# LayerNorm's scale split between x and the residual, a weight-conversion step on ScalarE, softmax reciprocals on GpSimd

## The chip, the cores and the metric

The kernel runs on one core of a Trainium2 chip. A core has five engines, each with its own in-order queue: TensorE (PE, with its weight loads shown as PEld), VectorE (DVE), ScalarE (ACT), GpSimd (POOL) and SyncE (SP), which here only issues DMAs. The metric is the device time of the one core in microseconds (us).

## The reference

Three stages on 8 x 576 = 4608 tokens, 512 wide:

```python
# 1 attention in blocks of 64 tokens, 8 heads of 64
scores = (1/8) * q_c @ k_c.T ; attn = exp(scores - max)
out = (attn / (sum(attn) + 1e-9)) @ v_c          # -> x [4608, 512]
# 2 LayerNorm, an MLP 512 -> 2048 -> 512, residual
xn = (x - mu) / sqrt(var + 1e-06) * g_ln
x2 = x + maximum(xn @ w_ch1, 0) @ w_ch2
# 3 gated MLP 512 -> 1024 -> 512 with a depthwise convolution over 3 tokens
h = maximum(x2 @ w_in, 0) ; c = conv3(h, conv_w)
y = (h * sigmoid(c)) @ w_out
```

q, k, v and g_ln arrive as float32, the four weights as 64-bit floats that the kernel turns into float32 itself.

## The kernel before

Tokens go in 36 tiles of 128 and in 9 slabs of 512 (four tiles). Every large product takes both operands as a high and a low part and adds three matmuls (`mm3`, lines 114 to 117): low*high, high*low, high*high. The first MLP product uses a two-by-two scheme with seven products, numbered 1 to 7, in place of eight; each slab has 28 slots (4 groups G of 7 products), and each product is 12 matmuls.

The program has three phases. In the first, attention for all tiles and the first MLP product; the result goes to DRAM (`hd`). In the second (`Down`, lines 719 to 746), the second product and the residual (`finish`, lines 812 to 820). In the third, the gated MLP (`Gate`).

What the change touches lies in the first phase. Before slab 0 can start, a start phase must do the attention of tiles 0 to 3 and convert half of the weights of `w_ch1`; the other half is converted during the first slots of slab 0. The order of the start is written out by hand in `START` (lines 18 to 41): each token is a letter and a number, up to `|` issued one after the other, and behind it in lists that run after slots 0, 1, 2, ... of slab 0. As engines are in order, this list is the order of each queue. The letters:

- `W` loads a 512 KB piece of a weight block (four blocks of four pieces; pieces 0 to 7 are needed for the start). `a` (ACT, line 135) takes the upper bits, `t` (line 141) the lowest three bits out of the low word, `m` (line 147) and `n` (line 153) put bits and sign together on DVE, `g` (ACT, line 313) multiplies by LayerNorm's weight, one value per partition from `g_sb`. `s` (DVE) makes the sums that the seven products need, `h` (ACT, line 338) and `l` (DVE, line 158) split into high and low.
- `L` loads q, k and v of a tile. `S` (PE) scores, `M` (DVE, lines 404 and 405) the maximum, `E` (ACT, line 414, eight instructions) the exponential with its row sums `sm`, `R` the reciprocals of the sums (lines 421 and 422), `P` (PE) transposes, `C` (ACT, line 434) copies out of PSUM, `V` (PE) times v, `X` (DVE, line 442) multiplies by the reciprocals, and queues the store of x to `xd` on SP.
- `B` LayerNorm's statistics (lines 452 to 455): mean and variance on DVE, the epsilon on DVE (line 454), the power -0.5 on POOL (line 455). `x` (in the list `y`; line 466) normalises. `T` (in the list `z`), `e`, `u`, `v` and `j` transpose and build the right-hand operands `xc`.

From tile 4 on, `session` (lines 667 to 712) places the same attention steps at fixed slots: V, S, M, X of two tiles at slot t, `E` and `B` and `x` at the slots after, `R`, `P` and `C` at t + 6. A product's PSUM bank is freed by a copy or a sum into `u` (lines 639 and 643 to 658); product 5 of the next group writes the bank that product 3 of the group before has left, and so waits for the sum at line 658.

SP issues DMAs in the order of the list too. The store of X2 stands ahead of `W9 W11 L4 W12`, that of X3 ahead of `W14 W13 W15 L5`.

Of the kernel before, what the change touches and what calls it, by code (L numbers as in the profile page):

```python
# [27 lines left out]
/ E5 g8 a9 t9 m10 n10
/ g10 a11 a12 t11 t12 m9
/ a14 n9 t14 g9 m12  # L30
/ R4 P4 C4 h14 n12 m11 g12 n11 a13
/ R5 P5 C5 l14 t13 g11 m14 h15
/ n14 s8 g14 l15 a15
# [11 lines left out]
def attn_moe_moe2(  # L45
# [226 lines left out]
    class Block:  # L272
# [37 lines left out]

        def g(self, i):
            kk = self.kk + 2 * (i % 2)
            nc.scalar.activation(out=self.y[i], in_=self.y[i], func=AF.Copy, scale=g_sb[:, kk:kk + 1])

        def s(self, i):
# [757 lines left out]
```

## Time and profile before

| | us |
|---|---|
| median of 3 runs | 1279.46 (1278.07 to 1280.18) |
| the profiled execution's own time | 1279.39 |
| its span | 1277.6 |
| PE busy | 1224.2 (96%) |
| DVE busy | 760.4 (60%) |
| ACT busy | 600.6 (47%) |
| POOL busy | 81.7 (6%) |

Busy shares are means over stages with different limits. The span in 40 slices of 32 us shows where PE is not full: only in the first three slices, in which the granted clock is lower too (tenths of full speed).

```profile
PE   5579999999999989999999999999999999999998
DVE  6996676576566568477632343334875655665540
ACT  6776556455464345244322222222765555565541
POOL 0000000000000000000000000000121111121100
PEclk6589999999999999999999999999999999999999
```

### The profile page before, as it was taken

What the parts mean: (1) busy time and instruction counts of PE and PEld (TensorE: products, weight loads), DVE (VectorE), ACT (ScalarE), POOL (GpSimd) and SP (SyncE); (2) the same over time, 40 slices, a digit from 0 to 9 for tenths busy, and PEclk for the clock granted to TensorE, in tenths of its full rate; (3) what the DMA queues carried; (4) which work ended last, traced back from release to release, by engine and by line L of the source; (5) the groups of instructions that cost most, each with busy time, mean ns of one, the idle gap of its engine ahead of it and who ended that gap; (6) DMA issues with size and microseconds to landing.
All of it is one profiled execution on the core that took longest, in us unless ns stands there. A gap on an engine that the chain in (4) does not pass through costs nothing.

```text
span 1277.6 us, 23149 instructions
## 1 busy us (share of the span) xinstructions
PE 1224.2 (96%) x8984; PEld 1069.8 (84%) x8984; DVE 760.4 (60%) x1458; ACT 600.6 (47%) x1482; POOL 81.7 (6%) x172
## 2 busy tenths in 40 slices
PE   5579999999999989999999999999999999999998
PEld 4469999999999987788888888888788888888887
DVE  6996676576566568477632343334875655665540
ACT  6776556455464345244322222222765555565541
POOL 0000000000000000000000000000121111121100
PEclk6589999999999999999999999999999999999999
DMA  9734766766685486676344445440121101111001
GB/s 263 214 109 150 264 225 223 257 231 232 217 265 202 159 301 224 204 247 231 124 149 153 157 152 181 157 164 34 33 66 59 50 25 58 63 38 41 25 25 50
DMA packets 145837, 192.37 MB, mean 151 GB/s; under 512 B 13632, under 2 KB 87360, under 8 KB 145728
## 3 DMA queue, kind: packets, MB, share of 16 engines
q1 hardware_dynamic: 145728, 190.91, 44.7%
q8 instruction: 70, 1.15, 0.4%
q14 instruction: 39, 0.32, 0.1%
HBM read 117.47 MB, written 73.40 MB: 149 GB/s over the span
## 4 chain that ended last, share of the span: by engine, by line
PE 82%; DVE 9%; DMA 3%; ACT 3%; SPq 1%; issue 1%; ACTq 0%; DVEq 0%
PE banks L115 27%; PE banks L116 26%; PE banks L117 26%; PE banks L388 3%; DMA w<-in_moe_w_ch_dram 1%; DVE mx L404 1%; PE banks L428 1%; DVE u L161 1%; DVE x L442 1%; DVE w L158 1%; DVE xc L158 1%; DMA wd<-in_moe_w_ch_dram 1%; DVE bs L452 1%; DVE hl L736 1%; DMA rk<-in_k_dram 1%
## 5 line engine op out<-in xcount | busy, mean ns | idle before, releaser
L115 PE MATMUL banks<-xc,w 128*128 128x256 f32 x1008 | 286.6, 284 | 13.2 <-DVE u L161 9.8
L116 PE MATMUL banks<-xc,w 128*128 128x256 f32 x1008 | 282.0, 280 | 0.0
L117 PE MATMUL banks<-xc,w 128*128 128x256 f32 x1008 | 281.8, 280 | 0.0
L736 DVE SCALAR_TENSOR_TENSOR hl<-hr,hh 128x512 fp32r<-128x512 f32 x144 | 99.2, 689 | 191.6 <-ACT hh L735 187.2
L735 ACT ACTIVATE hh<-hr 128x512 fp32r<-128x512 f32 x144 | 91.1, 632 | 257.2 <-PE banks L117 256.8
L115 PEld LDWEIGHTS banks<-xc,w 128*128 128x128 f32 x1008 | 192.9, 191 | 16.6 <-DVE u L161 7.3
L116 PEld LDWEIGHTS banks<-xc,w 128*128 128x128 f32 x1008 | 192.8, 191 | 0.0
L117 PEld LDWEIGHTS banks<-xc,w 128*128 128x128 f32 x1008 | 192.6, 191 | 0.0
L115 PE MATMUL banks<-w,hl 128*128 128x512 f32 x396 | 154.8, 391 | 0.0
L116 PE MATMUL banks<-w,hh 128*128 128x512 f32 x396 | 154.2, 389 | 0.0
L117 PE MATMUL banks<-w,hh 128*128 128x512 f32 x396 | 154.1, 389 | 0.0
L161 DVE TENSOR_TENSOR u<-banks,u 128x512 f32<-128x512 f32 x108 | 73.8, 684 | 77.5 <-ACT u L639 48.5
L956 DVE SCALAR_TENSOR_TENSOR cv<-hb,cw_sb,cv 128x510 f32<-128x510 f32 (+31 forms) x256 | 117.2, 512 | 0.6
L639 ACT COPY u<-banks 128x512 f32<-128x512 f32 x108 | 63.5, 588 | 113.5 <-PE banks L117 111.9
L115 PE MATMUL banks<-xb,w 128*128 128x512 f32 x288 | 112.7, 391 | 2.4 <-ACT hb L941 2.0
L117 PE MATMUL banks<-xb,w 128*128 128x512 f32 x288 | 112.1, 389 | 0.0
L116 PE MATMUL banks<-xb,w 128*128 128x512 f32 x288 | 112.1, 389 | 0.0
L414 ACT ACTIVATE pp<-banks,mx 128x64 f32<-128x64 f32 x288 | 87.0, 336 | 38.0 <-DVE x L442 32.4
L115 PEld LDWEIGHTS banks<-w,hl 128*128 128x128 f32 x396 | 74.3, 188 | 17.8 <-DVE hl L736 2.4
L943 POOL COPY hal<-hb 128x2 f32<-128x2 f32 x64 | 41.8, 652 | 727.9 <-ACT hb L941 727.9
L117 PEld LDWEIGHTS banks<-w,hh 128*128 128x128 f32 x396 | 74.3, 188 | 15.4
L116 PEld LDWEIGHTS banks<-w,hh 128*128 128x128 f32 x396 | 74.3, 188 | 15.2
(107 smaller groups left out, 2161.6 us busy)
## 6 DMA issues: line engine op xcount, KB each, us to landing
hd<-u SPq DMA_DIRECT2D x144, 256.0 KB, 3.9
hr<-hd SPq DMA_DIRECT2D x72, 512.0 KB, 3.8
w<-in_moe_w_ch_dram SPq DMA_DIRECT2D x27, 512.0 KB, 7.4
rv<-in_v_dram SPq DMA_DIRECT2D x36, 256.0 KB, 5.5
xd<-x SPq DMA_DIRECT2D x36, 256.0 KB, 2.1
xr<-xd SPq DMA_DIRECT2D x36, 256.0 KB, 3.8
x2d<-x2T SPq DMA_DIRECT2D x36, 256.0 KB, 2.0
x2r<-x2d SPq DMA_DIRECT2D x36, 256.0 KB, 3.9
```

What stands on the lines that cost most here:

```text
L115: nc.tensor.matmul(ps, ll, rh, start=first, stop=False, **kw)
L116: nc.tensor.matmul(ps, lh, rl, start=False, stop=False, **kw)
L117: nc.tensor.matmul(ps, lh, rh, start=False, stop=last, **kw)
L158: nc.vector.tensor_tensor(out=out, in0=a, in1=b, op=ALU.subtract)
L161: nc.vector.tensor_tensor(out=out, in0=a, in1=b, op=ALU.add)
L388: nc.tensor.matmul(ps[half(c), e, j, :], lt[half(e), j, c, :], rt[half(e), j, c, :], start=True, stop=True,)
L414: nc.scalar.activation(out=pp[:, j, e, :], in_=self.both[T][:, e, j, :], func=AF.Exp, scale=SCALE, bias=mx[:, e, j:j + 1], accum_out=sm[:, ...
L639: nc.scalar.copy(flat(t), bank[to])
L735: nc.scalar.activation(out=self.hh, in_=t, func=AF.Relu)
L736: nc.vector.scalar_tensor_tensor(out=self.hl, in0=t, scalar=0.0, in1=self.hh.bitcast(F32), op0=ALU.max, op1=ALU.subtract,)
L943: nc.gpsimd.tensor_copy(out=hal[:, f, :], in_=hb[:, 512:514])
L956: nc.vector.scalar_tensor_tensor(out=cv[:, a:e], in0=hb[:, a + tap:e + tap], scalar=cw_sb[:, tap, f:f + 1], in1=cv[:, a:e], op0=ALU.mult, ...
```

## The change

Four edits.

1. LayerNorm's weight is no longer multiplied into `w_ch1` on ACT (`g`, 16 instructions of 128x512, is gone). A tile `gain` holds the weight broadcast to 128 partitions (one DMA, at the new token `g0` behind `L3`), and `x` multiplies by it in place of 1/std, as a SCALAR_TENSOR_TENSOR. The DMA of `g_sb`, the first in SP's queue, is gone.
2. 1/std is kept for every tile in `rs_all` and multiplied in at the residual (`finish`): since 1/std is positive it passes through the maximum and the second product. `x` therefore no longer waits for POOL, and the epsilon is added on POOL too.
3. `t` for the blocks of `w_ch1` goes from DVE to ACT (`low_bits_act`).
4. `R` goes from DVE to POOL: an add and a power -1 over 128x8.

`s4` now shares a buffer with `t1` (room for `gain`), for which a few tokens near the end of the start (`u5`, `v5`, `u2`, `s7`, `u3`) stand in another order.

```diff
-R3 g7 y0 l5 C3 z0 y1 h9 V3 X2 W9 W11 L4 W12 e0 l9 g4 z1 X3 W14 W13 W15 L5 h8
+R3 y0 l5 C3 z0 y1 h9 V3 X2 W9 W11 L4 W12 e0 l9 z1 X3 W14 W13 W15 L5 h8
...
-    g_sb = const.tile([128, KD], F32, name="g_sb")
+    rs_all = const.tile([128, 64], F32, name="rs_all")
+    mone = const.tile([128, 2], F32, name="mone")
...
+    def low_bits_act(raw):
+        nc.scalar.activation(
+            out=raw[..., 0], in_=raw[..., 0].bitcast(U32), func=AF.Copy, scale=0.937 * 2.0 ** -29
+        )
...
         def t(self, i):
             if wide(w_ch1):
-                low_bits(self.raw[i])
+                low_bits_act(self.raw[i])
...
-        def g(self, i):
-            kk = self.kk + 2 * (i % 2)
-            nc.scalar.activation(out=self.y[i], in_=self.y[i], func=AF.Copy, scale=g_sb[:, kk:kk + 1])
...
-                self.s4 = at.tile([128, 512], "s4", 1)
+                self.s4 = at.tile([128, 512], "t1", 1)
...
         def R(self, T):
             sm = self.sm[T]
-            nc.vector.tensor_scalar_add(out=sm, in0=sm, scalar1=1e-9)
-            nc.vector.reciprocal(out=sm, in_=sm)
+            nc.gpsimd.tensor_scalar_add(out=sm, in0=sm, scalar1=1e-9)
+            nc.gpsimd.tensor_tensor(
+                out=sm, in0=sm, in1=mone[:, :, None].to_broadcast([128, 2, HP]), op=ALU.pow
+            )
...
-            rs = self.tile([128, 1], "rs", 2)
+            rs = rs_all[:, T:T + 1]
             nc.vector.bn_stats(out=bs, in_=self.xt[T].rearrange("p h d -> p (h d)"))
             nc.vector.bn_aggr(out=mv, in_=bs)
-            nc.vector.tensor_scalar_add(out=rs, in0=mv[:, 1:2], scalar1=1e-6)
+            nc.gpsimd.tensor_scalar_add(out=rs, in0=mv[:, 1:2], scalar1=1e-6)
             nc.gpsimd.tensor_tensor(out=rs, in0=rs, in1=mhalf, op=ALU.pow)
...
-            nc.vector.tensor_scalar(
-                out=to, in0=xt, scalar1=mv[:, 0:1], scalar2=rs, op0=ALU.subtract, op1=ALU.mult,
+            nc.vector.scalar_tensor_tensor(
+                out=to, in0=xt, scalar=mv[:, 0:1], in1=gain, op0=ALU.subtract, op1=ALU.mult,
             )
...
+            elif kind == "g":
+                nc.sync.dma_start(
+                    out=at.gain, in_=g_ln.rearrange("(o n) -> o n", o=1).broadcast_to([128, DM])
+                )
...
             for i in range(4):
-                plus(xr[i], down.acc[i], xr[i])
+                T = down.T[i]
+                nc.vector.scalar_tensor_tensor(
+                    out=xr[i], in0=down.acc[i], scalar=rs_all[:, T:T + 1], in1=xr[i], op0=ALU.mult,
+                    op1=ALU.add,
+                )
```

How the order moves is shown at three places of the start. The first is ACT around the exponentials of tile 1 (`pp,sm<-banks,mx`) up to the copy C1 (`pt<-banks`). L135 is `a`, L338 is `h`; a row ending in x8 stands for eight instructions. Before:

```order
L135 ACTIVATE w_401<-w_275 128x512
L414 ACTIVATE pp,sm<-banks,mx 128x64 x8
L135 ACTIVATE w_421<-w_277 128x512
L135 ACTIVATE w_401<-w_279 128x512
L338 CAST w_432<-w_417 128x512
L338 CAST w_436<-w_417 128x512
L434 COPY pt<-banks 128x512
```

and now (`a` is L136, `t` L148, `h` L340, `C` L439):

```order
L136 ACTIVATE w_400<-w_277 128x512
L148 ACTIVATE w_277<-w_277 128x512
L417 ACTIVATE pp,sm<-banks,mx 128x64 x8
L148 ACTIVATE w_279<-w_279 128x512
L136 ACTIVATE w_420<-w_279 128x512
L136 ACTIVATE w_400<-w_281 128x512
L148 ACTIVATE w_281<-w_281 128x512
L340 CAST w_431<-w_416 128x512
L340 CAST w_435<-w_416 128x512
L439 COPY pt<-banks 128x512
```

Between the exponentials of tile 1 and C1 stood two `a` and two `h`; now two `t` stand there as well, and one more `t` right ahead of the exponentials.

The second place is DVE from the statistics of tile 1 (`mv<-bs`) to the products X2 and X3 (`x<-banks,sm`). Before:

```order
L454 TENSOR_SCALAR rs<-mv 128x1
L421 TENSOR_SCALAR sm<-sm 128x8
L422 RECIPROCAL sm<-sm 128x8
L421 TENSOR_SCALAR sm<-sm 128x8
L422 RECIPROCAL sm<-sm 128x8
L466 TENSOR_SCALAR xn<-x,mv,rs 128x4x128
L158 TENSOR_TENSOR w_572<-w_304,w_572 128x512
L466 TENSOR_SCALAR xn<-x,mv,rs 128x4x128
L442 TENSOR_TENSOR x<-banks,sm 128x2x4x64
L158 TENSOR_TENSOR w_594<-w_421,w_594 128x512
L442 TENSOR_TENSOR x<-banks,sm 128x2x4x64
```

and now (BN_STATS and BN_AGGR are B1, L472 is `x`, L447 is `X`):

```order
L457 BN_STATS bs<-x 128x6
L458 BN_AGGR mv<-bs 128x2
L472 SCALAR_TENSOR_TENSOR xn<-x,mv,gain 128x4x128
L164 TENSOR_TENSOR w_567<-w_307,w_567 128x512
L472 SCALAR_TENSOR_TENSOR xn<-x,mv,gain 128x4x128
L447 TENSOR_TENSOR x<-banks,sm 128x2x4x64
L164 TENSOR_TENSOR w_588<-w_420,w_588 128x512
L447 TENSOR_TENSOR x<-banks,sm 128x2x4x64
```

The epsilon and the four instructions of R2 and R3 have left DVE's queue.

They stand on POOL now, at the third place. Before, POOL had only the 36 powers in phase one:

```order
masks.py:199 AFFINE_SELECT ident<-ident 128x128
L557 MEMSET mhalf 128x1
L562 MEMSET mhalf 128x1
L455 TENSOR_TENSOR rs<-rs,mhalf 128x1 x36
L943 COPY hal<-hb 128x2 x8
```

and now, from B0 (`rs_all<-mv`) over B1 to R2 and R3 (`sm`):

```order
L459 TENSOR_SCALAR rs_all<-mv 128x1
L460 TENSOR_TENSOR rs_all<-rs_all,mhalf 128x1
L459 TENSOR_SCALAR rs_all<-mv 128x1
L460 TENSOR_TENSOR rs_all<-rs_all,mhalf 128x1
L424 TENSOR_SCALAR sm<-sm 128x8
L425 TENSOR_TENSOR sm<-sm,mone 128x8
L424 TENSOR_SCALAR sm<-sm 128x8
L425 TENSOR_TENSOR sm<-sm,mone 128x8
```

R2 and R3 stand behind B1's epsilon and power, which wait for the variance of tile 1 from DVE.

## Rows read from the trace of the kernel before

**Rows 1.** Busy time by stretch: us, PE, PEld, DVE, ACT, POOL (instructions), clock, DMA

```profile
40.00:56.00 16.00, 6.07 (x54) 5.05 (x52) 15.61 (x29) 9.13 (x17) 1.41 (x2) 0.61 0.99 299
...
60.00:98.00 38.00, 27.06 (x308) 25.66 (x312) 35.23 (x73) 28.70 (x89) 1.79 (x2) 0.85 0.32 106
98.00:440.00 342.00, 338.87 (x4529) 334.74 (x4523) 223.97 (x472) 182.54 (x657) 21.05 (x30) 1.00 0.65 222
```

**Rows 2.** What PE waited for in the whole span: us, times, longest

```profile
PE banks L388 <- DMA rk<-in_k_dram: 14.0, 4, 7.8
PE banks L115 <- DVE u L161: 9.8, 9, 5.3
```

**Rows 3.** PE in order of time: start, us, what, idle before and releaser

```profile
58.24 1.65 PE L388 MATMUL banks<-rk,rq 64*64 64x64 f32 x32 [7.77 <-DMA rk<-in_k_dram]
...
84.49 0.58 PE L115 MATMUL banks<-xc,w 128*128 128x256 f32 x1 [5.35 <-DVE u L161]
```

**Rows 4.** Groups of instructions by shape: busy us, mean ns, idle before

```profile
L141 DVE TENSOR_SCALAR w<-w 128x512 int32<-128x512 uint32 x41 | 17.1, 422 | 7.2 <-DMA w<-in_moe_w_ch_dram 7.2
L313 ACT ACTIVATE w<-w,g_sb 128x512 f32<-128x512 f32 x16 | 11.8, 745 | 4.7 <-DVE w L153 4.7
L135 ACT ACTIVATE w<-w 128x512 f32<-128x512 f32 x16 | 10.7, 693 | 7.4 <-DMA w<-in_moe_w_ch_dram 7.4
L422 DVE RECIPROCAL sm<-sm 128x8 f32<-128x8 f32 x36 | 7.3, 203 | 1.2
L956 DVE SCALAR_TENSOR_TENSOR cv<-hb,cw_sb,cv 128x512 f32<-128x512 f32 x8 | 6.0, 751 | 0.3
```

**Rows 5.** SP's queue in order of time

```profile
0.73 0.74 SPq L558 DMA_DIRECT2D g_sb<-in_moe_g_ln_dram  x1
1.53 1.25 SPq L126 DMA_DIRECT2D w<-in_moe_w_ch_dram  x2
...
38.67 0.33 SPq L446 DMA_DIRECT2D xd<-x  x1
```

**Rows 6.** ACT in order of time, from the exponentials of tile 1 to C1

```profile
22.46 1.27 ACT L135 ACTIVATE w<-w 128x512 f32<-128x512 f32 x2
...
24.62 0.63 ACT L434 COPY pt<-banks 128x512 f32<-128x512 f32 x1
```

**Rows 7.** DVE in order of time: M2, B1's epsilon, R2, X2, X3

```profile
28.25 0.69 DVE L404 TENSOR_REDUCE mx<-banks 128x8 f32<-128x512 f32 x1 [0.19 <-PE banks L388]
...
35.60 0.15 DVE L454 TENSOR_SCALAR rs<-mv 128x1 f32<-128x1 f32 x1
35.67 0.16 DVE L421 TENSOR_SCALAR sm<-sm 128x8 f32<-128x8 f32 x1
...
37.96 0.68 DVE L442 TENSOR_TENSOR x<-banks,sm 128x512 f32<-128x512 f32 x1
...
39.26 0.69 DVE L442 TENSOR_TENSOR x<-banks,sm 128x512 f32<-128x512 f32 x1
```

**Rows 8.** POOL's lines 455, 940, 943: duration ns min/median/max, first and last start

```profile
L455 POOL TENSOR_TENSOR rs<-rs,mhalf x36: 548/715/928, 27.3 to 418.6; 128x1 f32<-128x1 f32 x36
...
L940 POOL COPY hb<-hal x64: 177/180/834, 912.0 to 1221.4; 128x2 f32<-128x2 f32 x64
...
L943 POOL COPY hal<-hb x64: 184/924/951, 881.6 to 1198.4; 128x2 f32<-128x2 f32 x64
```

**Rows 9.** ACT and DVE in order of time, in the conversion behind the start

```profile
65.17 0.73 ACT L313 ACTIVATE w<-w,g_sb 128x512 f32<-128x512 f32 x1 [0.38 <-DVE w L153]
...
73.00 0.69 DVE L161 TENSOR_TENSOR u<-banks,u 128x512 f32<-128x512 f32 x1 [0.91 <-ACT u L639]
...
83.75 0.68 DVE L161 TENSOR_TENSOR u<-banks,u 128x512 f32<-128x512 f32 x1
```

**Rows 10.** PE in a full slab, and DVE's residual in phase two

```profile
131.00 0.36 PE L115 MATMUL banks<-xc,w 128*128 128x256 f32 x1 [0.40 <-DVE u L161]
...
574.23 2.47 DVE L161 TENSOR_TENSOR xr<-banks,xr 128x512 f32<-128x512 f32 x4
```

More of the change, by code (lines that the diff above doesn't have):

```diff
@@ L18 @@
 START = """
-W0 W2 L0 W1 W3 L1 W4 W6 W5 W7 L2 L3 a0 t0 m0 n0 a2 t2 g0 m2 h0 n2 l0 g2
-S0 M0 a1 t1 E0 m1 n1 t3 a3 P0 R0 g1 m3 C0 n3 S1 h1 g3 l1 V0 M1 h2 a4 t4
+W0 W2 L0 W1 W3 L1 W4 W6 W5 W7 L2 L3 g0 a0 t0 m0 n0 a2 t2 m2 h0 n2 l0
+S0 M0 a1 t1 E0 m1 n1 t3 a3 P0 R0 m3 C0 n3 S1 h1 l1 V0 M1 h2 a4 t4
 E1 X0 s0 t6 s2 a6 s1 P1 a5 t5 s3 h4 R1 h3 m6 C1 l2 m5 V1 B0 S2 X1 W8 W10
-a7 t7 M2 m7 E2 n5 l3 S3 n6 m4 g5 P2 M3 g6 C2 n4 E3 V2 l4 n7 B1 h5 R2 P3
-R3 g7 y0 l5 C3 z0 y1 h9 V3 X2 W9 W11 L4 W12 e0 l9 g4 z1 X3 W14 W13 W15 L5 h8
-h7 B2 e1 B3 h6 u1 l7 v1 y3 l8 z3 s4 e3 y2 s6 z2 s5 e2 l6 h11 j0 u2 j1 u3
-s7 u5 v3 u7 h10 l11 j2 l10 u6 v2 h12 v6 j3 l12 u4 v5 h13 v4 l13 v7
+a7 t7 M2 m7 E2 n5 l3 S3 n6 m4 P2 M3 C2 n4 E3 V2 l4 n7 B1 h5 R2 P3
+R3 y0 l5 C3 z0 y1 h9 V3 X2 W9 W11 L4 W12 e0 l9 z1 X3 W14 W13 W15 L5 h8
+h7 B2 e1 B3 h6 u1 l7 v1 y3 l8 z3 s4 e3 y2 s6 z2 s5 e2 l6 h11 j0 u5 j1 u2 v5
+s7 u3 v3 u7 h10 l11 j2 l10 u6 v2 h12 v6 j3 l12 u4 h13 v4 l13 v7
 |
 S4 S5 M4 M5 E4 L6 L7 a8 t8 a10 t10 m8 n8
[L28 to L33, printed above, removed]
+/ E5 a9 t9 m10 n10
+/ a11 a12 t11 t12 m9
+/ a14 n9 t14 m12
+/ R4 P4 C4 h14 n12 m11 n11 a13
+/ R5 P5 C5 l14 t13 m14 h15
+/ n14 s8 l15 a15
 / h16 t15 s9 m13 l16 n13
-/ s10 g13 s11 h21 h17
+/ s10 s11 h21 h17
 / m15 h18 n15 l17 l21 l18
-/ g15 h19 h22 l19 s12
+/ h19 h22 l19 s12
 / h20 l22 l20 h23 s13 l23
@@ L358, in __init__ @@
             self.xs = {}
+            self.gain = self.tile([128, DM], "gain", 1)
         def tile(self, shape, tag, bufs):
@@ L450, in B @@
             mv = self.tile([128, 2], "mv", 2)
-            rs = self.tile([128, 1], "rs", 2)
+            rs = rs_all[:, T:T + 1]
             nc.vector.bn_stats(out=bs, in_=self.xt[T].rearrange("p h d -> p (h d)"))
             nc.vector.bn_aggr(out=mv, in_=bs)
-            nc.vector.tensor_scalar_add(out=rs, in0=mv[:, 1:2], scalar1=1e-6)
+            nc.gpsimd.tensor_scalar_add(out=rs, in0=mv[:, 1:2], scalar1=1e-6)
             nc.gpsimd.tensor_tensor(out=rs, in0=rs, in1=mhalf, op=ALU.pow)
-            self.mv[T] = mv, rs
+            self.mv[T] = mv
         def x(self, T):
-            mv, rs = self.mv.pop(T)
+            mv, gain = self.mv.pop(T), self.gain
             xn = self.xn[T] = self.tile([128, DM], "xn", 2)
@@ L464, in x @@
                 xt = xt.rearrange("p (g n) -> p g n", g=4)
+                gain = gain.rearrange("p (g n) -> p g n", g=4)
                 to = xn.rearrange("p (n g) -> p g n", g=4)
-            nc.vector.tensor_scalar(
-                out=to, in0=xt, scalar1=mv[:, 0:1], scalar2=rs, op0=ALU.subtract, op1=ALU.mult,
+            nc.vector.scalar_tensor_tensor(
+                out=to, in0=xt, scalar=mv[:, 0:1], in1=gain, op0=ALU.subtract, op1=ALU.mult,
             )
@@ L556, in attn_moe_moe2 @@
         make_identity(nc, ident)
+        nc.gpsimd.memset(mone, -1.0)
         nc.gpsimd.memset(mhalf, -0.5)
-        nc.sync.dma_start(out=g_sb, in_=g_ln.rearrange("(g G f) -> f g G", g=4, G=4))
         nc.scalar.activation(out=mhalf, in_=mhalf, func=AF.Exp, scale=0.0)
@@ L572, in one @@
             kind, i = step[0], int(step[1:])
-            if kind in "atmng":
+            if kind in "atmn":
                 getattr(blocks[i // 4], kind)(i % 4)
```

## The prediction

> **What bounds the kernel now.** I read the stretches first [rows 1]. From 98 to 440 us PE is busy 338.87 of 342 us at full clock; nothing on DVE, ACT or POOL can give much back there. Before 98 us it is not full: 6.07 of 16 us from 40 to 56, 27.06 of 38 from 60 to 98. DVE is: 15.61 of 16 and 35.23 of 38. So whatever the change is worth is decided in the first 98 us, and there the end is set by the time at which PE gets its operands, not by its work.
>
> Then the waits of PE [rows 2] and where they stand [rows 3]. The longest, 7.77 us up to 58.24, is S5 waiting for the keys of tile 5. Their DMA stands in SP's queue behind the store of X2, which goes out at 38.67, right after X2 [rows 5, 7]; from there the DMA engines carry the queued loads without a gap. So S5 follows X2, 20 us behind it. The second, 5.35 us up to 84.49, is product 5 waiting for DVE's sum of product 3 (83.75, the last row of [rows 9]). Before it DVE works through the conversion of the second half of the weights, with one gap of note: 0.91 us ahead of 73.00, where it waits for ACT's copy of product 7. So this stretch hangs on ACT until 73.00 and on DVE after it.
>
> **The change part by part.**
>
> *Front of the queue.* The DMA of g_sb goes; the first weight load is issued at 0.73 instead of 1.53 [rows 5]: 0.8 us earlier, and all loads behind it.
>
> *t on ACT.* A `t` on DVE took 0.42 us [rows 4]. The trace shows no `t` on ACT; the nearest row is `a`, which reads the other half of the same words: 0.69 us alone, and 0.58 apart when two follow (two take 1.27, [rows 6]). Bounds: 0.58 from the faster kinds of ACT work of this size, 0.75 from `g`; I take 0.58, and for `g`, which goes, 0.63 (0.745 less the same overlap of 0.11).
> Up to the exponentials of tile 1 ACT gains three `t` (1.7 us, those behind the first two pieces), loses two `g` (1.3) and starts 0.8 earlier, but must then wait for DVE's `n` of piece 3: I put its start at 0.1 later. Between these exponentials and C1 stood 24.62 - 22.46 = 2.16 us of work; two `t` make it 3.3. C1 comes 1.25 us later. Behind C1 hang V1 and, in PE's order, S2; M2 had waited only 0.19 us for S2 [rows 7], so M2 moves from 28.25 to about 29.5. DVE has by then lost its `t` work (0.42 each) and waits: the time saved on DVE before M2 is worth nothing, since ACT now carries it.
>
> *R and the epsilon on POOL.* From M2 to B1's variance DVE has no gap; 35.60 - 28.25 = 7.35, so the variance is there at 36.85. In DVE's queue R2, R3 (0.6 us) and the epsilon (0.07) are gone; X2 could start 0.6 us after its old time, at 38.55. But in POOL's queue R2 and R3 stand behind B1's epsilon and power, which need that variance. The chain is: epsilon, power of one column, add of 8 columns, power of 8 (R2), add, power (R3). POOL's power over one column takes 0.55 to 0.93, median 0.72 [rows 8]. A POOL instruction without arithmetic to speak of takes 0.18 where DVE is quiet and 0.92 in the median where it is busy: so an add costs between 0.18 and 0.95; I take 0.5 beside a busy DVE, 0.4 where DVE waits. The power over 8 columns is not in the trace. Low end 0.55: the columns cost nothing. High end 0.18 + 8 x 0.37 = 3.1: everything that the power takes over a copy, 0.55 - 0.18, is paid per column. I take 1.5, nearer to the row of one column, the only one of its kind.
> Variance 36.85, + 0.5 + 0.72 = 38.07, + 0.4 + 1.5: R2 is there at 40.0 and X2 moves from 37.96 to 40.0. + 0.5 + 1.5: R3 at 42.0, X3 moves from 39.26 to 42.0, 2.7 us. Behind X3 DVE is full up to M4 [rows 1], so M4 and the exponentials behind it are 2.7 us late; S5 follows X2 and is 2.0 late.
>
> The Trainium skill, GPSIMD Engine Reference, section 4.1 (Engine selection), sets elementwise work on GpSimd at about twice VectorE's time for instructions of two inputs. By that, R (0.16 + 0.20 on DVE) would take 0.7 us on POOL, R3 would be ready at 39.5, before DVE asks for it: this is the first rival. The row speaks against it: one column of power takes 0.72 where DVE's reciprocal of eight takes 0.20.
>
> *Conversion, 60 to 98 us.* Behind the exponentials of tile 4 ACT is full up to the copy of product 7, but for 0.38 us [rows 9]. In that run it loses five `g` (3.15) and gains seven `t` (4.06), and the 0.38 closes: + 0.5. So DVE's sum at 73.00 comes at 2.7 + 0.5 later, whatever DVE has saved until there; its seven `t` and R4, R5 turn into a longer wait than the 0.91. After it, to 83.75, DVE loses one `t` (0.34 from start to start) and one epsilon (0.07): - 0.4. Product 5 starts 2.8 us later than 84.49. From there to 98 DVE leads still, and loses only 0.07; R6 and R7 stand too late in it to matter.
>
> *g0, x and the shared buffer.* The broadcast of `gain` (256 KB) is issued behind L3, about 10 us before x0 reads it. It lies in the gap that the DMA queue leaves until X2. `x` with two inputs costs up to 0.75 (L956, a form with a pointer, [rows 4]) against 0.54 to 0.75 now; in slabs it lies between other work, and it no longer waits for POOL. The moved u5 and v5 keep ACT's and DVE's counts: nothing.
>
> *Slabs.* Once in each of seven periods PE waits 0.40 us for a sum [rows 10] in front of which DVE has M, X, M, X, B and two sums without a gap. Of these the epsilon goes: 7 x 0.08 = - 0.5. R in the slabs has seven slots of the 28 between the last exponential and X; hidden unless POOL takes several us for each.
>
> *Residual.* Four sums of 0.68 (2.47 together, [rows 10]) become the pointer form: 0.75, + 0.07 each, 0.27 a slab. Between nothing and 9 x 0.27 = 2.4; DVE is tight only in the two slabs in which it converts weights too: + 0.5.
>
> Sum: + 2.8 - 0.5 + 0.5 = + 2.8. The profiled execution took 1279.39 us, 0.07 under the median. Forecast 1282.2.
>
> **Rivals.**
> *GpSimd is quick* (R2 and R3 are not awaited, eight columns hardly more than one). Not slower. X3 then moves only by the 0.6 of M2: + 0.6 + 0.5 - 0.4 - 0.5 + 0.5 = + 0.7: 1280.1. For it: 0.55 is the low bound. It decides where an add and a power take under 0.9 us together.
> *GpSimd is slow*: 0.95 for an add and 3.1 for a power. R2 at 36.85 + 0.95 + 0.93 + 4.05 = 42.8, R3 at 46.8; X3 + 7.6, - 0.4 for POOL's free stretches, + 0.5 - 0.4 - 0.5 + 0.5: 1286.7. For it: POOL's copies go from 0.18 to 0.92 beside DVE.
> *ACT has room, DVE's time is given back whole.* On the other side: 14 `t` of 0.42 (the first two hide behind DMAs) and six R of 0.34 are 7.9 us: 1271.5 with the slabs and the residual as above. For it: DVE is 93 to 98% busy in both stretches and ACT under 76%. Against it: the ACT work lies exactly ahead of C1 and of product 7's copy, and M2 had only 0.19 us to give. It decides if C1 and the copy of product 7 come no later than before.
>
> **How the numbers follow.** Forecast 0.43, quick GpSimd 0.27, slow GpSimd 0.13, ACT with room 0.17. What a measurement can tell from no change is 0.2%, 2.6 us: 1276.9 to 1282.0. The forecast lies at its upper edge, with a range of its own of 1280.5 to 1284: 0.26 of it slower, 0.17 within. Quick GpSimd: 0.24 within, 0.02 faster, 0.01 slower. Slow: 0.13 slower. ACT with room: 0.15 faster, 0.02 within. Together faster 0.17, within 0.43, slower 0.40. The range 1273 to 1287 takes in the rivals but for the outer half of the fast one and a third of the slow one.
>
> **What would show it.** C1 at about 25.9 instead of 24.62 and M2 at 29.5, with DVE idle for 1 us before it; X2 waiting for POOL to about 40.0, X3 to 42.0; S5 at about 60.2; DVE idle for 3 us or more ahead of the sum of product 7, at about 76; PE's wait for product 3's sum ending near 87; PE's seven short waits down to 0.32. Wrong if X2 is not awaited from POOL, if M2 comes no later than before, or if the wait of product 5 shrinks by several us.

## The result, and the profile after

The changed kernel takes 1289.22 us (median of 4 runs, 1285.37 to 1289.43) against 1279.42 (4 runs, 1278.07 to 1280.18): a ratio of 1.0068, 95% interval 1.0056 to 1.0081. It is slower, as forecast, but by 9.8 us where 2.8 were forecast, and outside the range. The profiled execution took 1289.33 us, its span is 1287.5 against 1277.6.

Three marks in the two traces tell where the 9.9 us of span went. The first product behind S6 and S7 starts at 103.47 instead of 101.54 (+1.9). PE's wait for the last copy of the slabs ends at 463.56 instead of 455.74, so the slabs take 5.9 more. The first transpose of the last residual starts at 888.69 instead of 878.82: 2.1 more in between. From there to the end both take 398.8. Before:

```profile
101.54 0.58 PE L115 MATMUL banks<-xc,w 128*128 128x256 f32 x1
...
455.74 0.38 PE L115 MATMUL banks<-xc,w 128*128 128x256 f32 x1 [2.96 <-ACT u L639]
...
878.82 0.70 DVE L818 STREAM_TRANSPOSE x2T<-xr 128x512 f32<-128x512 f32 x1
```

and now:

```profile
103.47 0.58 PE L116 MATMUL banks<-xc,w 128*128 128x256 f32 x1
...
463.56 0.58 PE L116 MATMUL banks<-xc,w 128*128 128x256 f32 x1 [2.80 <-ACT u L649]
...
888.69 0.70 DVE L832 STREAM_TRANSPOSE x2T<-xr 128x512 f32<-128x512 f32 x1
```

**The start.** What PE waited for in the whole span, as in [rows 2]: what, us, times, longest. Before, for `x` and for ScalarE's copies:

```profile
PE banks L474 <- DVE xn L466: 4.4, 2, 3.7
...
PE banks L115 <- ACT u L639: 3.4, 3, 3.0
```

and now:

```profile
PE banks L480 <- DVE xn L472: 8.5, 3, 6.8
...
PE banks L391 <- DMA rk<-in_k_dram: 7.9, 3, 6.2
PE banks L116 <- ACT u L649: 6.4, 3, 3.4
PE banks L116 <- DVE u L167: 5.2, 2, 3.6
```

Waits for `x` (L472) and for ScalarE's copies have grown. The rows behind them, in order of time, answer to [rows 6 and 7]: M0 and M1 on DVE, C1 on ACT, M2 and the end of B1's variance on DVE, POOL's queue, X2 and X3 on DVE.

```profile
9.09 0.68 DVE L407 TENSOR_REDUCE mx<-banks 128x8 f32<-128x512 f32 x1
...
17.45 0.68 DVE L407 TENSOR_REDUCE mx<-banks 128x8 f32<-128x512 f32 x1
...
24.22 0.62 ACT L439 COPY pt<-banks 128x512 f32<-128x512 f32 x1
...
26.97 0.69 DVE L407 TENSOR_REDUCE mx<-banks 128x8 f32<-128x512 f32 x1
...
34.12 0.18 DVE L458 BATCH_NORM_AGGREGATE mv<-bs 128x2 f32<-128x6 f32 x1
...
34.39 0.90 POOL L459 TENSOR_SCALAR rs_all<-mv 128x1 f32<-128x1 f32 x1 [8.45 <-DVE mv L458]
35.37 0.90 POOL L460 TENSOR_TENSOR rs_all<-rs_all,mhalf 128x1 f32<-128x1 f32 x1
36.36 0.51 POOL L424 TENSOR_SCALAR sm<-sm 128x8 f32<-128x8 f32 x1
36.95 1.67 POOL L425 TENSOR_TENSOR sm<-sm,mone 128x8 f32<-128x8 f32 x1
...
38.66 0.69 DVE L447 TENSOR_TENSOR x<-banks,sm 128x512 f32<-128x512 f32 x1 [1.76 <-POOL sm L425]
...
38.71 0.25 POOL L424 TENSOR_SCALAR sm<-sm 128x8 f32<-128x8 f32 x1
39.04 1.67 POOL L425 TENSOR_TENSOR sm<-sm,mone 128x8 f32<-128x8 f32 x1
...
40.74 0.69 DVE L447 TENSOR_TENSOR x<-banks,sm 128x512 f32<-128x512 f32 x1 [0.80 <-POOL sm L425]
```

X2 and X3 wait for POOL, as the prediction said: from M2 to X3 it is 13.77 us instead of 11.01 [rows 7], where the prediction had 12.5. These rows stand 1.3 to 2.5 us earlier than forecast, since the first loads of this execution came early: M0 starts at 9.09, in the kernel before at 12.61, and in the profiles of all kernels below anywhere between 8.9 and 13.0. M0 and M1 of the kernel before:

```profile
12.61 0.69 DVE L404 TENSOR_REDUCE mx<-banks 128x8 f32<-128x512 f32 x1 [0.86 <-PE banks L388]
...
19.14 0.69 DVE L404 TENSOR_REDUCE mx<-banks 128x8 f32<-128x512 f32 x1
```

So times of the start are compared from mark to mark, not from zero. Counted from M1 the start has lost 3.6 us (below); that the first product behind S6 and S7 is only 1.9 later is in part this early start.

The conversion behind the start, as in [rows 3 and 9]: S5 on PE, three `m` and the sums of products 7 and 3 on DVE, product 5 on PE.

```profile
58.51 1.51 PE L391 MATMUL banks<-rk,rq 64*64 64x64 f32 x32 [6.23 <-DMA rk<-in_k_dram]
...
63.46 0.69 DVE L153 SCALAR_TENSOR_TENSOR w<-w,w 128x512 int32<-128x512 int32 x1 [2.47 <-ACT w L148]
...
68.03 0.69 DVE L153 SCALAR_TENSOR_TENSOR w<-w,w 128x512 int32<-128x512 int32 x1 [1.21 <-ACT w L148]
...
70.22 0.69 DVE L153 SCALAR_TENSOR_TENSOR w<-w,w 128x512 int32<-128x512 int32 x1 [0.77 <-ACT w L148]
...
75.44 0.69 DVE L167 TENSOR_TENSOR u<-banks,u 128x512 f32<-128x512 f32 x1 [1.28 <-ACT u L649]
...
85.66 0.69 DVE L167 TENSOR_TENSOR u<-banks,u 128x512 f32<-128x512 f32 x1
...
86.40 0.39 PE L116 MATMUL banks<-xc,w 128*128 128x256 f32 x1 [3.55 <-DVE u L167]
```

S5 follows X2 by 19.85 us, as the prediction has it. DVE's gap ahead of the sum of product 7 is 1.28 us instead of 0.91, not 3 or more; but ahead of it DVE waits three times for `t` itself (L148), 4.45 us in all, so the wait on ACT that the prediction expected is there, in pieces. PE's wait for product 3's sum has shrunk from 5.35 to 3.55, since PE itself came later.

**The slabs.** Against [rows 1], PE's stretch is no less full, its clock is at the full level, and DVE has less to do:

```profile
98.00:440.00 342.00, 339.73 (x4466) 335.46 (x4467) 215.61 (x379) 181.53 (x656) 98.84 (x117) 1.00 0.65 221
```

The seven waits of 0.40 us [rows 10] are gone from the list of PE's waits, and yet the slabs are longer. The products themselves come further apart. PE in order of time, around the transposes of P at 154.32 (such a place, at which the attention of the next two tiles begins, is called a turn here):

```profile
133.02 0.28 PE L118 MATMUL banks<-xc,w 128*128 128x256 f32 x1
133.32 0.35 PE L116 MATMUL banks<-xc,w 128*128 128x256 f32 x1
...
146.26 0.29 PE L117 MATMUL banks<-xc,w 128*128 128x256 f32 x1
...
154.20 0.28 PE L118 MATMUL banks<-xc,w 128*128 128x256 f32 x1
154.32 1.03 PE L433 MATMUL banks<-ident,pp 128*128 128x128 f32 x8
...
155.31 0.28 PE L117 MATMUL banks<-xc,w 128*128 128x256 f32 x1
...
170.63 0.28 PE L118 MATMUL banks<-xc,w 128*128 128x256 f32 x1
```

From 146.26 to 154.20 there are 70 steps from one product to the next, 0.1134 us each; from 155.31 to 170.63 there are 130 of 0.1178. No row between shows a wait. Cut into groups of 12 such steps, the slabs fall on two levels, 113.5 and 117.8 ns in the mean, with hardly a group between; a handful that hold a wait lie above. The kernel before has 4 groups in the slow spacing and 184 in the fast one; the changed kernel has 149 and 33. 145 groups more, of 12 x 4.25 ns, are 7.4 us. With the steps outside whole groups it is more: between the marks all steps from one product to the next without a wait add up to 300.6 us before and to 309.2 now, 8.7 more. At each of the seven waits the step was 0.68 us long, as from 130.32 to 131.00 [rows 10]:

```profile
130.32 0.28 PE L117 MATMUL banks<-xc,w 128*128 128x256 f32 x1
```

Now it is 0.30 (133.02 to 133.32 is one): 2.7 come off in all. The last wait of the slabs is 0.2 shorter. 8.7 - 2.7 - 0.2 = 5.8, against the 5.9 of the marks.

A spacing lasts over products, over V and S, until it changes at P's transposes or behind a wait. In the changed kernel each second turn, as the one at 154.32, ends in the slow one; at the others it goes over from the one to the other.

**Behind the slabs.** The residual's rows, and the clock behind the wait that ends at 463.56 (window, busy PE, PEld, DVE, ACT, POOL with counts, granted clock, DMA):

```profile
L825 DVE SCALAR_TENSOR_TENSOR xr<-banks,rs_all,xr x36: 741/744/751, 540.2 to 888.0; 128x512 f32<-128x512 f32 x36
```

```profile
463.00:469.00 6.00, 5.44 (x25) 5.44 (x26) 3.17 (x6) 3.78 (x8) 0.00 (x0) 0.50 0.79 262
```

Four residual sums take 2.72 us instead of 2.47 [rows 10], and PE waits for `hl` four times, 1.2 us, instead of once, 0.3. The rest of the 2.1, 1.2 us, is lost before the first residual sum, with the clock: it was granted at 0.50 (1.2 GHz) for these 6 us, behind that wait, where the kernel before shows 0.72 over its own 6:

```profile
455.00:461.00 6.00, 5.26 (x31) 5.26 (x32) 4.14 (x7) 4.88 (x10) 0.00 (x0) 0.72 0.95 312
```

PE had stood idle for about as long in both, 2.80 and 2.96 us. From this wait to the first residual sum the profiles below take between 74.6 and 76.7 us (here 76.6, before 75.4), and the longest is `g_later`, whose instructions there are those of the kernel before. So nothing ties the 1.2 us to the change.

### The profile page after: what moved, and what is told of

Its sections match the earlier page's. It is cut to its first block, busy times and chain, and to the rows that moved or that the text cites. A ratio compares the mean times of both kernels' runs of the same rounds, so it can differ in the third digit from the quotient of the medians.

```text
span 1287.5 us, 23152 instructions
## 1 busy us (share of the span) xinstructions
PE 1232.7 (96%) x8984; PEld 1078.0 (84%) x8984; DVE 752.4 (58%) x1334; ACT 599.5 (47%) x1482; POOL 181.3 (14%) x281
## 4 chain that ended last, share of the span: by engine, by line
PE 84%; DVE 7%; ACT 4%; DMA 3%; issue 1%; SPq 1%; POOL 0%; ACTq 0%; DVEq 0%
PE banks L116 27%; PE banks L118 27%; PE banks L117 27%; PE banks L391 2%; DMA w<-in_moe_w_ch_dram 1%; DVE w L164 1%; PE banks L433 1%; ACT pp L417 1%; DMA wd<-in_moe_w_ch_dram 1%; DVE xr L825 1%; DVE hl L746 1%; ACT w L148 0%; DMA x2d<-x2T 0%; ACT w L136 0%; DVE xc L164 0%
## 5 line engine op out<-in xcount | busy, mean ns | idle before, releaser
L116 PE MATMUL banks<-xc,w 128*128 128x256 f32 x1008 | 290.7, 288 | 11.7 <-ACT u L649 6.4
L118 PE MATMUL banks<-xc,w 128*128 128x256 f32 x1008 | 285.8, 283 | 0.0
L117 PE MATMUL banks<-xc,w 128*128 128x256 f32 x1008 | 285.7, 283 | 0.0
```

The lines of the kernel that those rows point to most:

```text
L116: nc.tensor.matmul(ps, ll, rh, start=first, stop=False, **kw)
L117: nc.tensor.matmul(ps, lh, rl, start=False, stop=False, **kw)
L118: nc.tensor.matmul(ps, lh, rh, start=False, stop=last, **kw)
```

## The experiments

"Groups" are those of 12 products in the slabs, slow and fast, of the profiled execution, one for each kernel. Theories: I first held that GpSimd's powers beside the transposes throw PE into the slow spacing (T); its rivals were the lost waits (S) and the place of the weights in memory (P). "LayerNorm's part" is the change without its edits to `t` and `R`.

**R back on VectorE** (`r_vector`)

```
-            nc.gpsimd.tensor_scalar_add(out=sm, ...); nc.gpsimd.tensor_tensor(out=sm, ..., op=ALU.pow)
+            nc.vector.tensor_scalar_add(out=sm, ...); nc.vector.reciprocal(out=sm, in_=sm)
```

> The changed kernel with the softmax reciprocals (R) back on VectorE; all else as changed. The changed kernel took 1289.2 us against 1279.4; by its profile 2.1 us are lost before 98 us, 5.7 us from there to the end of the slabs, where the start-to-start spacing of the 128x256 products is 0.118 us instead of 0.113 for most of the time, and 2.1 us behind. Theory T (the power on GpSimd runs while PE does the transposes at the turn of a session, and PE's stream comes out of it in the slow spacing): the spacing goes back to 0.113 and 5 to 6 us come back; with some 0.7 us at the start for X2 and X3 that no longer wait for GpSimd, 1282 to 1284 us. Theory S (the wait of 0.40 us in each period kept the stream fast; the epsilon that left VectorE took it away): R does not lie between M and the sum that PE waits for, so the slow spacing stays; only the start gains: 1288 us. Theory P (the spacing follows where the tiles lie in memory since gain was added): as S, 1288 us.

1287.74 us (1286.98 to 1291.12), ratio 1.0067 (1.0048 to 1.0086); groups 133 slow, 52 fast. T falls. Beside the rest of the change R on GpSimd costs 1.5 us by the medians, which the two intervals do not tell from nothing.

**R earlier in the slabs** (`r_early`)

```
-                for T in tss:                   # in turn
-                    at.R(T)
+                on(t + 3 + 2 * i, lambda T=T: at.R(T))
```

> The changed kernel with R still on GpSimd, but in the slabs issued one slot behind the exponentials of its own tile (slots 3 and 5 of a session) and not with the transposes of slot 6. Theory T: the powers are over before the transposes, the spacing stays at 0.113, 5 to 6 us come back: 1283 to 1285 us. Theory G (any work of GpSimd in the slabs slows the stream, wherever it lies): no gain, 1289. Theories S and P: no gain, 1289.

1288.55 us (1286.72 to 1290.68), 156 slow and 26 fast. T falls here too.

**LayerNorm alone** (`norm_alone`): R as in `r_vector`, and

```
-                low_bits_act(self.raw[i])
+                low_bits(self.raw[i])
```

> Only the LayerNorm part of the change: weight multiplied into x, 1/std at the residual, epsilon on GpSimd; t and R stay on VectorE. Theory T: fast spacing in the slabs; the start gains 1.4 us from the load queue that lost g_sb and the g steps, and loses 0.4 us for each x of the first tiles: 1278 to 1280 us. Theory P, and S if the epsilon is what counts: slow spacing, 1284 to 1286.

1284.01 us (1283.41 to 1285.20), ratio 1.0032 (1.0020 to 1.0044); 118 slow, 68 fast. The slow spacing comes with LayerNorm's part, without any GpSimd power in R. Its start costs nothing: from M1 to the sum of product 3 it takes 64.09 us, the kernel before 64.61.

**t back on VectorE** (`t_vector`): of the two edits of `norm_alone` the second alone.

> The changed kernel with the third conversion step (t) back on VectorE. All theories: the slabs stay as slow as in the changed kernel. Of the start: VectorE gets 14 steps of 0.42 us back, ScalarE loses 14 of 0.58; the sum of product 7 at 75.44 us no longer waits for ScalarE's copy. My reading of the profile (ScalarE set this stretch): 1 to 2 us faster than the changed kernel, 1287 to 1288. Rival (VectorE sets it, its 5.9 us of t come back into the chain): 1291 to 1295.

1284.37 us (1282.12 to 1287.02, 8 runs), 114 slow and 71 fast. By the medians `t` on ScalarE costs 4.8 us beside the rest of the change, and 3.7 without R (`norm_alone` to `r_vector`): more than I read from the wait of 1.28 us alone. Not all of it is `t`: the profiles of these pairs differ by 35 and by 15 slow groups too, 1.8 and 0.8 us. From M0 to the sum of product 3 `t` costs 3.6 us (76.57 and 72.99) and 3.4 (73.83 and 70.45). R without `t` costs 0.4 (`norm_alone` to here).

**Weights moved by 256 bytes** (`pad_256`): `+ const.tile([128, 64], F32, name="pad")` in the kernel before.

> The kernel before with one unused tile of 256 bytes per partition among the constants: no instruction differs, all weights of the products (and what lies behind them on the same side) stand 256 bytes further on, as they do in the changed kernel since rs_all; the operands xc, and the buffers of the attention, stay. LayerNorm's part alone already brought the slow spacing (118 runs of 12 products out of 186 at 0.118 us) and 4.3 us between the first product and the end of the slabs. Theory P (it is where the weights lie against the operands): slow spacing here too, 1283 to 1285 us. Theory N (it is something that the LayerNorm part does: longer x, epsilon on GpSimd, or attention's own buffers, which moved by 2112 bytes): spacing of 0.113, 1279 to 1280.

1278.85 us (1277.93 to 1282.02, 10 runs), ratio 1.0002 (0.9991 to 1.0014); 12 slow, 177 fast. The place of the weights alone does not bring the slow spacing.

**Weights put back** in the changed kernel (`after_replaced`) and in LayerNorm's part (`norm_replaced`): 

```
-    rs_all = const.tile([128, 64], F32, name="rs_all")
+        rs_p = tc.alloc_tile_pool(name="rs", bufs=1, reuse_waits="tile")    # behind wa
+        rs_all = rs_p.tile([128, 64], F32, name="rs_all")
```

> The changed kernel with rs_all in a pool of its own behind the weights and mone in the tile of mhalf, so that the weights stand where they stood in the kernel before; no instruction differs. Theory P: spacing of 0.113 in the slabs, 4 to 6 us come back: 1283 to 1285 us, what is left being the start (2.1 us) and the phase behind the slabs. Theory N: 1289 us.

> LayerNorm's part alone, with the weights where they stood before (rs_all behind them). Its run without that: 1284.0 us, of which the first product came 1.65 us earlier than in the kernel before and the slabs took 4.3 us more. Theory P: 1278.5 to 1280 us, about the kernel before or a little faster. Theory N: 1284 us.

1287.28 us (147 slow, 41 fast) and 1284.39 us (168 slow, 18 fast): theory P, with the weights, falls.

**R and t without LayerNorm** (`r_t_alone`): the kernel before with both edits of the change.

> The kernel before with R on GpSimd and t on ScalarE, but LayerNorm and its g steps as before, and the weights where they stood. Both theories: spacing of 0.113. The runs with one part undone put t at 3 to 4.5 us and R at 1 to 1.5, nearly all in the first 100 us: 1283 to 1285 us if their costs do not hang on the LayerNorm part; with g still on ScalarE (14 steps of 0.63 us beside the 14 of t) ScalarE could cost more: up to 1288.

1288.35 us (1287.72 to 1293.95), ratio 1.0073 (1.0048 to 1.0098), with 26 slow and 158 fast. Here the loss is mostly the start: the sum of product 7 stands 59.96 us behind M1 instead of 53.86. ScalarE with 16 `g` and 16 `t`, and R on GpSimd, cost 8.0 us against the 1280.34 of the kernel before in the same session; without the `g` steps the same two edits cost 5.2 (`norm_alone` to the changed kernel). So taking the `g` steps away seems to spare `t` some of its cost, which no run shows by itself.

Left for the slow spacing are the places of attention's buffers (theory A), the epsilon on GpSimd (E) and the longer `x` (X).

**The instructions of before, every buffer where LayerNorm's part puts it** (`at_shift`); a few steps of the start stand in the changed kernel's order.

```
+            self.gain = self.tile([128, DM], "gain", 1)      # not used
-                self.s4 = at.tile([128, 512], "s4", 1)
+                self.s4 = at.tile([128, 512], "t1", 1)
-            rs = self.tile([128, 1], "rs", 2)
+            rs = rs_all[:, T:T + 1]
```

> The kernel before with its instructions (but for two steps of slab 0 in another order at the start, since s4 shares the buffer of t1), and every buffer where it stands in the LayerNorm part alone: an unused gain moves q, k, v, the exponentials pp, pt and x by 2112 bytes, xn and bst by 2048, rs_all moves the weights by 256. Theory A (places of the attention's buffers): slow spacing in half of the slabs or more, 1283 to 1285 us. Theory E (the epsilon on GpSimd) and theory X (x with two inputs, 0.72 instead of 0.54 us) both: spacing of 0.113 as in the kernel before, 1279 to 1281.

1285.48 us (1285.16 to 1287.32), ratio 1.0052 (1.0037 to 1.0067); 180 slow, 2 fast. 12 us of one long stretch behind a second turn, this kernel:

```profile
200.00:212.00 12.00, 12.00 (x104) 12.00 (x103) 6.38 (x10) 4.35 (x8) 0.00 (x0) 1.00 0.63 219
```

and the kernel before in the same stretch of a period:

```profile
199.00:211.00 12.00, 12.00 (x108) 12.00 (x108) 6.00 (x10) 4.60 (x8) 0.00 (x0) 1.00 0.67 234
```

PE is busy without a gap in both, at full clock, with 104 products in one and 108 in the other. The old instructions at the new places are slow, so neither E nor X is needed; with `pad_256` it is the places of attention's buffers, theory A. No edit has taken its waits away (there are seven, 1.5 us in all), so theory S is not needed either.

**gain taken late** (`gain_late`): LayerNorm's part, so that `q`, `k`, `v`, `pp`, `pt` and `x` lie as before.

```
-            self.gain = self.tile([128, DM], "gain", 1)      # in __init__
+                at.gain = at.tile([128, DM], "gain", 1)      # in step g0, now behind X0
+            self.tile([128, 1], "rs", 2)                         # in B, kept but not used
```

> LayerNorm's part alone with gain taken (and loaded) behind X0, so that q, k, v, pp, pt and x stand where they stood in the kernel before; xn and bst stay 2048 bytes further on. Theory A, if pp, pt or x count: fast spacing, and with the earlier start 1278 to 1280 us. Theory A, if xn or bst count, theories E and X: slow spacing, 1284 us.

1279.10 us (1275.69 to 1283.61, 10 runs), ratio 0.9999 (0.9984 to 1.0015); 33 slow, 157 fast. 4.9 us less than `norm_alone`, with the same instructions, of which the load of `gain` comes later. It has the epsilon on GpSimd and `x` with its second input, and is fast: E and X do not bring the slow spacing by themselves.

**x without its second input** (`norm_x_short`, which leaves LayerNorm's weight out of the result) and **the epsilon on VectorE** (`norm_eps_vector`), both on LayerNorm's part.

```
-            nc.vector.scalar_tensor_tensor(out=to, in0=xt, scalar=mv[:, 0:1], in1=gain, ...)
+            nc.vector.tensor_scalar(out=to, in0=xt, scalar1=mv[:, 0:1], scalar2=mone[:, 0:1], ...)  # 1.0
```

```
-            nc.gpsimd.tensor_scalar_add(out=rs, in0=mv[:, 1:2], scalar1=1e-6)
+            nc.vector.tensor_scalar_add(out=rs, in0=mv[:, 1:2], scalar1=1e-6)
```

> LayerNorm's part alone with x as a subtraction and a multiplication by one: LayerNorm's weight is left out of the result. x falls back to about 0.54 us in the slabs. Theory X: fast spacing; with some 0.4 us less for each early x, 1278 to 1280. Theories A and E: slow spacing, 1283 to 1284.

> LayerNorm's part alone with the epsilon back on VectorE: the wait of 0.4 us in each period should be there again in full. Theory E: fast spacing, 1279 to 1280. Theories A and X: slow spacing, 1284.

1279.21 us with 92 slow, 97 fast, and 1285.80 us with 175 slow, 9 fast. Theory E falls again. The first alone would not settle X: half of its groups are slow still, and its early `x` take 0.70 to 0.77 us instead of 1.10 to 1.23, which saves in the start as well: 62.32 us from M1 to the sum of product 3 instead of 64.09.

**64 bytes.** The change drops the two small `rs` tiles of attention's pool, 64 bytes with their padding, and adds `gain`, 2048 in the place of `s4`. `after_64` keeps the two tiles in the changed kernel, unused; `before_64` puts 64 spare bytes at the end of the pool of the kernel before.

```
+            self.tile([128, 1], "rs", 2)        # after_64, in B
+                at.tile([128, 16], "spare", 1)      # before_64, ahead of t1
```

> The changed kernel with 64 spare bytes kept in attention's pool (the two tiles of rs, unused): its buffers from gain to x stand 64 bytes lower than in the changed kernel, 2048 bytes and not 2112 above those of the kernel before; no instruction differs. Theory A64 (the 64 bytes decide: where pp, pt and x lie within 128 bytes): fast spacing, 4 to 5 us come back: 1284 to 1285 us. Theory A2048 (the larger step, which part of memory the buffers lie in): slow spacing, 1288 to 1289.

> The kernel before with 64 spare bytes at the end of attention's pool: all its buffers stand 64 bytes lower; no instruction differs. Theory A64: slow spacing, 1283 to 1285 us. Theory A2048: fast spacing, 1279 to 1280.

`after_64`: 1284.21 us (1279.46 to 1286.59, 10 runs), ratio 1.0035 (1.0022 to 1.0049), 39 slow, 144 fast: 5.0 us back for two tiles that nothing uses (4.2 by the two ratios). In the compiled kernels every instruction and every wait of it is that of the changed kernel; the places alone differ. `before_64`: 1279.52 us, 9 slow, 178 fast. The 64 bytes decide in the one and not in the other.

**The same 64 bytes in the kernel before** (`rs_apart`): `pp` to `x` rise by 64, `xn` and `bst` stay.

```
-            rs = self.tile([128, 1], "rs", 2)
+            rs = rs_all[:, T:T + 1]
```

> The kernel before with 1/std in rs_all instead of the two small tiles of attention's pool: these tiles go, and q, k, v, pp, pt and x stand 64 bytes higher, as they do in the changed kernel but for its 2048; xn and bst stay; no instruction differs. Of the slow spacing it is known that pp up to x 64 bytes lower in the changed kernel end it (after_64), and that all buffers 64 bytes lower in the kernel before don't bring it (before_64). Theory D (the distance between pp to x and xn or bst decides, or where both lie within 128 bytes: in all slow kernels both are at 96): slow spacing, 1283 to 1285 us. Theory O (it takes the place that the whole step of 2112 bytes gives): fast, 1279 to 1280.

1284.66 us (1282.64 to 1286.77), ratio 1.0042 (1.0025 to 1.0060); 140 slow, 43 fast.

```profile
200.00:212.00 12.00, 12.00 (x104) 12.00 (x103) 5.06 (x8) 4.72 (x9) 0.00 (x0) 1.00 0.67 234
```

This is 5.2 us for the removal of two 4-byte tiles. No instruction that computes has changed but for the place of 1/std; POOL has also lost 33 waits for a free `rs` tile, as in `at_shift`, but `after_64` and `gain_late` have none of these either and are fast. Addresses in the compiled kernels: `pp` at 147232 and `xn` at 161760 in the kernel before, 149344 and 163808 in the changed one, 147296 and 161760 here, 149280 and 163808 in `after_64`, 147168 and 161696 in `before_64`. In the kernels so far in which the slow spacing leads, both are at 96 modulo 128; in those in which the fast one leads by far, one is at 96 and one at 32. `norm_x_short`, with both at 96, lies between (92 and 97). So theory D (where the two lie against each other within 128 bytes) fits the runs so far, but the last run below does not obey it. Whether the distance or the two residues count, and why PE, whose products read neither, keeps a spacing from it, was not tried and stays open.

**The change with its buffers in place** (`after_gain_late`): the whole change, `gain` taken late.

> The changed kernel, whole, with gain taken behind X0, so that q, k, v, pp, pt and x stand where they did in the kernel before. It shows what the change costs without the slow spacing. By adding (LayerNorm's part so placed 1279.1 us, R and t together 5.2 more in the pair 1284.0 and 1289.2): 1284 us, R on GpSimd and t on ScalarE being the whole of the loss. Rival (placement is all of it, the parts of the start hide in each other): 1280 to 1281.

1282.80 us (1279.62 to 1286.70, 10 runs), ratio 1.0023 (1.0010 to 1.0036); 64 slow, 120 fast. 6.4 us less than the changed kernel by the medians, 5.8 by the two ratios. The profile is of the longest run, 1286.70. Its start, where M0 stands at 11.72: C1 26.27, M2 29.02, X2 40.71 (behind 1.76 us for POOL), X3 42.79 (0.80 for POOL) and the sum of product 7 77.49 (1.28 for ScalarE): the waits are those of the changed kernel.

**The load of g_sb later** (`g_later`), in the kernel before: a step `q0` that issues it.

```
-W0 W2 L0 W1 W3 L1 W4
+W0 W2 L0 q0 W1 W3 L1 W4
```

> The kernel before with the load of g_sb behind the loads of tile 0 and not ahead of all; a candidate for a faster kernel. My first step (the front of the queue) read 0.8 us from the issues: 1278.6 us. Rival: the start hangs on when the first loads land, which differs by 2 us and more between profiles of one kernel, so that nothing can be seen: 1279.4.

1279.24 us (1277.14 to 1281.95, 10 runs), ratio 1.0001 (0.9988 to 1.0013): the front term can't be seen by itself.

**LayerNorm's statistics one slot later** (`stats_later`), in the slabs of the kernel before:

```
-                on(t + 1 + i, lambda T=T: at.B(T))
-                on(t + 3 + i, lambda T=T: at.x(T))
+                on(t + 2 + i, lambda T=T: at.B(T))
+                on(t + 4 + i, lambda T=T: at.x(T))
```

> The kernel before, in whose slabs LayerNorm's statistics (B) and x come one slot later: a candidate for a faster kernel. In each of seven periods PE waits 0.40 us for a sum in front of which VectorE has one B (1.0 us); with B behind that sum the wait goes if nothing else takes its place: 2.8 us, 1276.5 us. Rival (a later sum is then late by as much, since VectorE's work in the period is the same): 1279.4. Second rival (without the wait the stream falls into the slow spacing): 1283.

1273.17 us (12 runs), ratio 0.9961 (0.9941 to 0.9981): faster than both kernels, and by the medians 6.3 us faster than the one before, where 2.8 were expected. Ten runs lie from 1270.97 to 1276.49, two at 1281.83 and 1285.18. The profile is of the one at 1281.83, with 193 groups slow and 6 fast. PE's waits from 98 to 470 us in it:

```profile
PE banks L115 <- ACT u L639: 2.5, 1, 2.5
PE banks L115 <- DVE u L161: 0.7, 1, 0.7
```

The seven waits are gone. This execution is in the slow spacing from the first product on, and stays in it, though every buffer lies where the kernel before has it, `pp` at 32 and `xn` at 96. So the places are not all: they weigh on which spacing leads, but do not settle it for an execution, and the waits, with which the spacing can change, may have a part in it, as the second rival had it. 193 groups of 12 x 4.25 ns are 9.8 us: in the fast spacing the same trace would end near 1272, where the ten runs lie. That these ten ran in the fast spacing is inferred; none of them was profiled.

## Why the prediction was wrong, step by step

**Front of the queue, -0.8.** The first step on weights starts 1.46 us earlier in this pair of profiles (4.44 and 5.90), but M0 differs by more than that between the profiles anyhow, and `g_later` shows nothing.

**t on ACT.** C1 comes 6.77 us after M1 instead of 5.48: 1.29 more, 1.25 were forecast. M2, though, moved by only 0.41 from M1, not by 1.25: from C1 to M2 it is 2.75 us instead of 3.63. Not seen was that `t` also lies ahead of M1 (M0 to M1: 8.36 instead of 6.53; 7.55 to 8.55 in the seven profiles with `t` on ScalarE, 6.25 to 7.58 in the others), and that from X3 to the sum of product 7 it adds 0.96 net, not 0.5. By the marks `t` is 3.4 to 3.6 us of the start, more than `x` (1.8) or R (0.4 to 1.5) cost.

**R behind B1's epsilon and power.** The mechanism is the one forecast, the size was not: from M2 to X3 2.76 us more, where 1.5 were forecast. From the variance to R2's end the prediction had 0.5 + 0.72 + 0.4 + 1.5 = 3.1 us; the rows have 0.90 + 0.90 + 0.51 + 1.67 and 4.2 with the gaps. The power of 8 columns is 1.68 in the median, near the 1.5 chosen, and eight times DVE's reciprocal [rows 4]; the adds and the power of one column beside a busy DVE are what came out longer. The Trainium skill (GPSIMD Engine Reference, section 4.1, Engine selection) puts elementwise work with two inputs on GpSimd at about twice VectorE's time; taken for R as in the prediction's first rival, the rows decide otherwise, as the prediction held. VectorE's own power was not run. What the runs pay for R is less than its chain: 0.4 us without `t`, 1.5 with it.

**Sum of the start.** From M1 to the sum of product 3: 64.61 us before, 68.21 after, +3.6; the forecast for product 5 was +2.8. The parts are +0.41 to M2, +2.76 to X3, +0.96 to the sum of product 7 and -0.53 to that of product 3, where the prediction had +1.25, +1.5, +0.5 and -0.4: M2 too much and R too little, which partly cancel. With its buffers in place the whole change takes 1282.80, ratio 1.0023 with an interval that is 1.3 to 4.6 us, around the forecast 1282.2. So this path held, and the sum of the instructions' prices came near. That it came so near is in part luck: in the profile of that kernel the start is 3.9 us longer and 60 groups more are slow.

**g0, x and the shared buffer, "nothing".** This step failed, twice. `x` takes 0.72 to 0.75 us in the slabs, but up to 1.19 early, where up to 0.75 was allowed for; `norm_x_short` puts that at 1.8 us of the start:

```profile
L472 DVE SCALAR_TENSOR_TENSOR xn<-x,mv,gain x36: 718/744/1193, 34.2 to 426.1; 128x512 f32<-128x512 f32 x36
```

And I asked of the new and the dropped tiles when they are read and written, not what they shift. The pool lost two tiles and gained one, and that costs 5.0 (`after_64`) to 6.4 us (`after_gain_late`) by the medians, 4.2 to 5.8 by the ratios: about half of the 9.8 or more, where the prediction put nothing. How a place does this stays open.

**Slabs, -0.5.** "Nothing on DVE, ACT or POOL can give much back there" took PE's own pace as fixed. The waits shrink more than forecast (2.7 us come off, and in `after_64` six of about 0.2 us are left, 1.3 in all), but the pace of the products is worth up to 4%, 8.7 us here.

**Residual, +0.5.** 2.72 us for four instead of 2.47, as forecast; the waits for `hl` grew by 0.9. The other 1.2 us behind the slabs are the clock, which nothing ties to the change.

**Rivals.** GpSimd slow (1286.7) is closest in time and still not it: with R back on VectorE 1287.7 us remain. GpSimd quick and ACT with room are refuted by the waits of X2, X3 and of the sum of product 7.

## What to carry to other kernels

Where PE is full, compare the start-to-start spacing of a repeated matmul at the same granted clock in both traces before looking for waits: a stretch can lose 4% with no idle row. An edit that adds or drops a tile, however small, moves what lies beside it; a kernel with the old instructions and the new places, or one with the dropped bytes put back, prices that by itself. Profile more than one execution where such a spacing is in play: one profile shows one of them. And a price of instructions that holds for the path says nothing yet of the total.

## What the runs showed of the hardware

Products of 128x256 run at 113.5 or 117.8 ns from start to start at a granted clock of 1.00, each for tens of us at a time. Which of the two led moved with 64 bytes in the places of buffers that the products do not read (149 slow groups in the changed kernel, 39 in `after_64`), but not with them alone (`stats_later`). On GpSimd a power over 8 columns took 1.68 us against 0.58 over one (the medians of this trace), so by estimate a column more costs about 0.16:

```profile
L425 POOL TENSOR_TENSOR sm<-sm,mone x36: 1673/1676/5022, 14.8 to 412.8; 128x8 f32<-128x8 f32 x36
...
L460 POOL TENSOR_TENSOR rs_all<-rs_all,mhalf x36: 577/578/1237, 25.4 to 425.6; 128x1 f32<-128x1 f32 x36
```

A DVE instruction with pointer and second input took 0.74 us in the slabs, and 1.11 to 1.19 where the output is written in steps of four elements.
